# A banded-attention and two-block kernel on one core: the recorded list of order changes gets 59 more entries

## The chip, the cores and the metric

The kernel runs on one core of a Trainium2 chip. The time is the device time of one execution in microseconds (us), the median of several runs. The core has five engines with a queue of instructions each: TensorE (PE, matrix products), VectorE (DVE), ScalarE (ACT), GpSimd (POOL), and SyncE (SP), which here only starts transfers. An engine takes its own instructions in order. It stops at one whose input is not yet there, and everything behind that instruction waits too.

## The reference

Three steps follow each other for 4 batches of 576 positions and 512 channels (8 heads of 64).

```python
# 1. attention in a band of 128 positions, with a distance bias per head
scores = np.where(mask, scale * q @ k.T + bias, -1e9)      # mask: 0 <= i - j < 128
attn = exp(scores - max); attn /= sum;  x = attn @ v       # heads side by side: 512 channels
# 2. first block: 512 -> 1024 -> 512
h = maximum(x @ w_in, 0)
x = (h * sigmoid(conv3(h))) @ w_out                        # 3 taps per channel, centred
# 3. second block: 512 -> 512 -> 512
x = (sigmoid(conv5(x)) * (x @ w_val)) @ w_out2             # 5 taps per channel, causal
```

All data are fp32.

## The kernel before

**Tiling.** The work is cut into 8 units: each of the 4 batches has two parts of its positions (4 or 5 blocks of 64 rows in the first part). For a unit the steps are: attention, `hidden` (product with `w_in`, relu, 3-tap convolution, gate), `mixed` (product with `w_out` and the 5-tap convolution), `valued` (product with `w_val`, times the gate), `output` (product with `w_out2`). While one unit goes through the two blocks, the attention of the next is mixed in between. Channels lie on the 128 partitions, positions along the free axis, so that a tile is 128 x 254 to 128 x 322.

**Products of split numbers.** An fp32 matrix is held as a rounded "hi" part and the remainder "lo". A product is three matmuls: hi by hi, hi by lo, lo by hi (L1026, L1027, L1028; the first block of the later units uses halves of 16 bits, L1020). So every product needs its input split first. `cast` makes hi (L474 on ACT, L475 on DVE, L476 on POOL), `sub` makes lo (L508 on DVE, L509 on POOL).

**Work around the products.** Banded scores are matmuls (L802, L940). Then come a row minimum on DVE (L751), exp on ACT (L756), one over the row sum in two steps, a tiny one on POOL (L760) and a reciprocal on DVE (L762), a scaling of the rows (L817 POOL, L819 ACT, L823 DVE; in the later units L969 ACT or L971 DVE makes hi of it and L973 lo), a transposition (L829, or a transfer), and the product with v (L856, L1001). The taps of the convolutions are multiply-adds on DVE (L491), or a scaled copy on ACT (L501) that POOL adds (L502). `scaled` copies with a factor on ACT (L484) or DVE (L485). The weights come by transfers of 512 KB into a ring of three raw tiles and are unpacked by `widen`: L530 (DVE), L532 (ACT), L541 (DVE), then hi on ACT (L547) or POOL (L548) and lo on POOL (L509). A raw tile's next transfer can start only when its reader is through.

**What sets the order.** Each operation is entered once, with its inputs, outputs, length and the engines it may run on. A planner (`Program`, L84 to L260) then makes one order per engine: `forward` walks through the plan and gives each engine the ready operation of the smallest priority. `JOLTS` is a tuple of seeds. For each seed in turn `jolt` picks a stretch of 10, 30 or 60 us of the plan, adds random noise to the priorities of the operations in it, picks another engine for some of those that may run on several, changes how long some matmul groups of the attention are held back, and runs `forward` again. The result for one seed is the start of the next.

**Fillers.** Where the plan leaves PE free before 80 us, `warm` (L1239) puts small matmuls that nobody reads into PE's queue. Their number follows from the plan.

Of the kernel before, what the change touches and what calls it, by code (L numbers as in the profile page):

```python
# [37 lines left out]
NATIVE = ()  # L38
LATE = (11,)
HALF = {"in": 2, "out": 4}  # L40
# [1274 lines left out]
```

## Time and profile before

| | before |
|---|---|
| time, median of 3 runs | 402.96 us (402.84 to 403.02) |
| profiled execution: its own time | 402.0 us |
| profiled execution: span of the core | 400.2 us |
| PE busy | 385.5 us (96%), 3915 matmuls |
| DVE busy | 338.0 us (84%), 1041 instructions |
| ACT busy | 301.1 us (75%), 919 instructions |
| POOL busy | 239.3 us (60%), 365 instructions |
| granted TensorE clock | 1.00 in every stretch |

Busy shares are averages over the span. What matters for an order is the idle time: on which engine, at which place, and for whom the engine waited there. The number in square brackets in a timeline row is this idle time, with the instruction that ended it.

### The profile page before, as it was taken

Reading aid. Unit: us, or ns where it says so; the run is one execution under the profiler, and the core shown is the slowest. Engines: PE = TensorE matmul, PEld = TensorE weight load, DVE = VectorE, ACT = ScalarE, POOL = GpSimd, SP = SyncE. Lnnn points to the kernel's source line nnn. Section 1 sums busy time; section 2 is a strip of 40 time slices with the busy share of each in tenths; the row PEclk is TensorE's granted clock in tenths of the full one; section 3 lists DMA queues with packets and bytes.
Section 4 is the critical chain, followed back from the end, with each engine's and each line's share of the span. In section 5 each row is a group of like instructions: output and inputs, shape, how many; then the busy total and the mean of one; then the engine's idle time right before and its main releaser. Section 6 shows DMA issues by size and latency. Waiting matters only on the chain.

```text
span 400.2 us, 10946 instructions
## 1 busy us (share of the span) xinstructions
PE 385.5 (96%) x3915; PEld 336.3 (84%) x3915; DVE 338.0 (84%) x1041; ACT 301.1 (75%) x919; POOL 239.3 (60%) x365
## 2 busy tenths in 40 slices
PE   8898999999999998999999999999999999999996
PEld 7678988899998877999899866799878877798886
DVE  3999999999889989988879998986989778945591
ACT  4989999858797796758977987768877769714661
POOL 3677998947769737744476867353555248532631
PEclk9999999999999999999999999999999999999999
DMA  7977678753544474706692564707284620301001
GB/s 250 314 242 292 233 249 278 245 156 66 168 102 125 149 171 118 181 12 191 94 186 42 179 146 118 175 7 204 75 166 62 119 55 2 63 19 67 2 0 55
DMA packets 64919, 53.79 MB, mean 134 GB/s; under 512 B 44512, under 2 KB 57184, under 8 KB 64864
## 3 DMA queue, kind: packets, MB, share of 16 engines
q1 hardware_dynamic: 64864, 53.08, 49.2%
q8 instruction: 31, 0.51, 0.5%
q14 instruction: 24, 0.20, 0.2%
HBM read 38.51 MB, written 4.72 MB: 108 GB/s over the span
## 4 chain that ended last, share of the span: by engine, by line
PE 65%; DVE 16%; ACT 8%; DMA 5%; issue 3%; POOL 2%; SPq 1%; POOLq 0%; DVEq 0%; ACTq 0%
PE pm L1020 18%; PE pm L1026 13%; PE pm L1027 12%; PE pm L1028 12%; DVE t L491 4%; PE pss L940 3%; PE pss L1001 2%; DMA raw<-in_vN 2%; DVE pss L751 2%; DMA raw<-in_w_val 1%; PE pss L802 1%; DVE gts L491 1%; DVE gts L541 1%; DVE raw L530 1%; ACT pss L756 1%
## 5 line engine op out<-in xcount | busy, mean ns | idle before, releaser
L1020 PE MATMUL pm<-xh,hin 128*128 128x320 f16 (+1 forms) x504 | 68.5, 286 | 0.4 <-DVE t L491 0.3
L1020 PEld LDWEIGHTS <-hin 128*128 128x128 f16 x504 | 48.1, 97 | 14.6 <-issue 1.3
L1020 PEld LDWEIGHTS <-hout 128*128 128x128 f16 x384 | 37.0, 97 | 13.0 <-issue 2.1
L502 POOL TENSOR_TENSOR gts<-gts,t 128x317 f32<-128x317 f32 (+3 forms) x36 | 29.2, 820 | 28.6 <-ACT t L501 17.7
L1026 PE MATMUL pm<-g,wout 128*128 128x254 f32 (+3 forms) x128 | 39.4, 308 | 2.0 <-DVE t L491 1.5
L1026 PE MATMUL pm<-g,wval 128*128 128x318 f32 (+3 forms) x128 | 39.9, 312 | 0.6 <-ACT gts L1128 0.2
L1026 PE MATMUL pm<-g,wo 128*128 128x318 f32 (+3 forms) x128 | 39.3, 307 | 0.0
L1027 PE MATMUL pm<-g,wval 128*128 128x318 f32 (+3 forms) x128 | 38.1, 298 | 0.0
L1028 PE MATMUL pm<-g,wout 128*128 128x254 f32 (+3 forms) x128 | 37.8, 296 | 0.2 <-POOL wout L509 0.2
L1027 PE MATMUL pm<-g,wout 128*128 128x254 f32 (+3 forms) x128 | 38.0, 297 | 0.0
L1027 PE MATMUL pm<-g,wo 128*128 128x318 f32 (+3 forms) x128 | 37.9, 296 | 0.0
L1028 PE MATMUL pm<-g,wo 128*128 128x318 f32 (+3 forms) x128 | 37.7, 294 | 0.0
L1028 PE MATMUL pm<-g,wval 128*128 128x318 f32 (+3 forms) x128 | 37.6, 294 | 0.0
L751 DVE CUSTOM_DVE_ANT_0 pss<-pss,bm 128x192 f32<-128x192 f32 (+2 forms) x90 | 30.6, 349 | 7.3 <-PE pss L802 5.5
L756 ACT ACTIVATE pss<-pss,st 128x192 f32<-128x192 f32 (+2 forms) x81 | 30.3, 375 | 7.7 <-DVE st L751 7.1
L491 DVE SCALAR_TENSOR_TENSOR t<-pm,wcc,t 128x318 f32<-128x318 f32 (+3 forms) x56 | 28.3, 512 | 5.6 <-ACT t L484 3.6
L509 POOL TENSOR_TENSOR g<-gts,g 128x318 fp32r<-128x318 f32 (+3 forms) x26 | 21.3, 827 | 18.3 <-DVE g L475 9.2
L1077 ACT ACTIVATE t<-t 128x318 f32<-128x318 f32 (+3 forms) x64 | 28.4, 446 | 4.1 <-DVE t L491 3.6
L491 DVE SCALAR_TENSOR_TENSOR t<-t,pm 128x318 f32<-128x318 f32 (+3 forms) x64 | 28.3, 448 | 2.7 <-ACT t L1077 2.5
L973 DVE SCALAR_TENSOR_TENSOR pp<-pss,st,pp 128x192 f16<-128x192 f32 (+2 forms) x79 | 27.7, 388 | 2.0 <-ACT pp L969 1.6
L491 DVE SCALAR_TENSOR_TENSOR t<-pm,cc,t 128x254 f32<-128x254 f32 (+7 forms) x56 | 27.6, 511 | 0.7 <-ACT t L484 0.5
L1067 ACT ACTIVATE pm<-pm,wsc 128x320 f32<-128x320 f32 (+1 forms) x42 | 20.1, 478 | 10.1 <-PE pm L1020 9.7
(195 smaller groups left out, 1304.4 us busy)
## 6 DMA issues: line engine op xcount, KB each, us to landing
raw<-in_w_out SPq DMA_DIRECT2D x12, 512.0 KB, 4.2
raw<-in_w_in SPq DMA_DIRECT2D x8, 512.0 KB, 4.5
qkt<-in_qk SPq DMA_DIRECT2D x10, 384.0 KB, 4.1
vr<-in_vN SPq DMA_DIRECT2D x36, 96.0 KB, 3.0
qkt<-in_qk SPq DMA_DIRECT2D x6, 480.0 KB, 4.1
pp<-in_qk SPq DMA_DIRECT2D x6, 480.0 KB, 4.5
raw<-in_vN SPq DMA_DIRECT2D x6, 384.0 KB, 3.3
pp<-in_qk SPq DMA_DIRECT2D x6, 384.0 KB, 4.5
```

The source lines that it names most:

```text
L491: pg.add("DVE", dve_t(n, 0 if isinstance(scalar, float) else 1), lambda: nc.vector.scalar_tensor_tensor(out=out, in0=in0, scalar=scalar, i ...
L502: pg.add("POOL", pool_t(n, True), lambda: nc.gpsimd.tensor_tensor(out=out, in0=out, in1=t, op=ALU.add), prio, (tk,), (key,))
L509: "POOL": (pool_t(n, True), lambda: nc.gpsimd.tensor_tensor(out=lo, in0=src, in1=f32(hi), op=ALU.subtract))}
L751: pg.add("DVE", 75 + 1.05 * nkey, lambda: nc.vector.tensor_tensor_reduce(out=s, in0=s, in1=tab[:, 192 - nkey:192], op0=ALU.add, op1=ALU.mi ...
L756: pg.add("ACT", act_t(nkey, True, 2), lambda: nc.scalar.activation(out=to, in_=s, func=AF.Exp, scale=-1.0, bias=best, accum_out=total), pr ...
L973: pg.add("DVE", dve_t(nkey, 1), lambda sc=sc, hi=hi, lo=lo, ri=ri: nc.vector.scalar_tensor_tensor(out=lo, in0=sc, scalar=ri, in1=hi, op0=A ...
L1020: return [nc.tensor.matmul(out=o, lhsT=a, rhs=b_, start=first and i == 0, stop=last and i == 2) for i, (a, b_) in enumerate(((wh, hi), (wh ...
L1026: return [nc.tensor.matmul(out=o, lhsT=wh, rhs=hi, start=first, stop=False), nc.tensor.matmul(out=o, lhsT=wh, rhs=lo, start=False, stop=Fa ...
L1027: nc.tensor.matmul(out=o, lhsT=wh, rhs=lo, start=False, stop=False),
L1028: nc.tensor.matmul(out=o, lhsT=wl, rhs=hi, start=False, stop=last)]
L1067: pg.add("ACT", act_t(Nx, True, 1 if half else 0) + 35, lambda h=h: nc.scalar.activation(out=h[:, 0:Nx], in_=h[:, 0:Nx], func=AF.Relu, sca ...
L1077: pg.add("ACT", act_t(Ng), lambda c=c: nc.scalar.activation(out=c, in_=c, func=AF.Tanh, scale=0.5), pr, (), (ak,))
```

## The change

The tuple `JOLTS` gets 59 more seeds behind the 60 that it had. Nothing else in the file changes; later lines move down by 6 (L509 becomes L515, L760 becomes L766).

```diff
-    30003181, 30003414, 30003574, 30003667, 30003669)
+    30003181, 30003414, 30003574, 30003667, 30003669, 50000130, 50000253, 50000317, 50000349, 50000423, 50000450,
...
+    220004046)
```

The operations, tiles and transfers stay the same 2731. What changes is their order on each engine and, for some, the engine. Counting the built programs: ACT goes from 777 to 768 instructions, DVE from 1018 to 1031, POOL from 370 to 366, SP keeps 232. PE loses 20 fillers (111 to 91) and keeps every matmul that is read. The engines change for these operations:

| operation | before | after |
|---|---|---|
| `cast` ACT / DVE / POOL | 69 / 6 / 37 | 66 / 8 / 38 |
| `sub` DVE / POOL | 7 / 113 | 11 / 109 |
| hi of the row scaling, L969 ACT / L971 DVE | 89 / 15 | 84 / 20 |
| row scaling, L819 ACT / L817 POOL | 18 / 16 | 20 / 14 |
| hi of a weight, L547 ACT / L548 POOL | 14 / 10 | 13 / 11 |
| relu, L1067 ACT / L1069 DVE | 58 / 6 | 56 / 8 |

On PE 460 of 494 groups of matmuls keep their order among each other, and none moves by more than 6 places. The order is unchanged from 81 to 180 us and from about 320 to 330 us of the profiled execution of before.

Three places follow, each before and after. A row has the line, the kind, and output<-inputs with the shape.

**First place:** POOL at about 51 to 57 us of before, while the weights are unpacked and the second unit's attention starts. `st0` holds row sums, `pp` the exponentials, `wout` the weights `w_out`, `gts` what `widen` unpacks into, `x` the attention's output.

```order
L729 CAST x2_130<-x2_130 128x2x4
L729 CAST x3_131<-x3_131 128x2x4
L509 TENSOR_TENSOR wout140_89<-gts_141,wout040_81 128x512
L502 TENSOR_TENSOR t8_140<-t8_140,t0_132 128x253
L817 TENSOR_SCALAR pp_192<-pp_192,st0_190 128x192
L760 TENSOR_SCALAR st0_190<-st0_190 128x2
L548 TENSOR_SCALAR wout050_82<-gts_141 128x512
L760 TENSOR_SCALAR st0_190<-st0_190 128x1
L817 TENSOR_SCALAR pp_192<-pp_192,st0_190 128x192
L509 TENSOR_TENSOR g6_123<-t7_139,g6_123 128x254
L817 TENSOR_SCALAR pp_192<-pp_192,st0_190 128x192
L509 TENSOR_TENSOR wout150_90<-gts_141,wout050_82 128x512
```

```order
L735 CAST x2_130<-x2_130 128x2x4
L508 TENSOR_TENSOR t8_140<-t8_140,t0_132 128x253
L515 TENSOR_TENSOR wout140_89<-gts_141,wout040_81 128x512
L823 TENSOR_SCALAR pp_192<-pp_192,st0_190 128x192
L554 TENSOR_SCALAR wout050_82<-gts_141 128x512
L766 TENSOR_SCALAR st0_190<-st0_190 128x2
L515 TENSOR_TENSOR wout150_90<-gts_141,wout050_82 128x512
L823 TENSOR_SCALAR pp_192<-pp_192,st0_190 128x192
L766 TENSOR_SCALAR st0_190<-st0_190 128x1
L515 TENSOR_TENSOR g6_123<-t7_139,g6_123 128x254
```

The remainder of `wout150` moved up by four operations, and both tiny operations on `st0` moved behind a longer one.

**Second place:** POOL at about 288 to 298 us, in `hidden` and `mixed` of a later unit. `ghout` are the hi and lo halves of the gated hidden rows, `v16` and `vr` the values of the next attention (`vr` is filled by a transfer).

```order
L476 TENSOR_SCALAR v16_179<-vr_178 128x640
L760 TENSOR_SCALAR st1_191<-st1_191 128x6
L476 TENSOR_SCALAR ghout30_168<-t7_139 128x258
L908 TENSOR_TENSOR v16_179<-vr_178,v16_179 128x640
L509 TENSOR_TENSOR ghout30_168<-t7_139,ghout30_168 128x258
L509 TENSOR_TENSOR ghout40_169<-t0_132,ghout40_169 128x258
L502 TENSOR_TENSOR t3_135<-t3_135,t4_136 128x258
L509 TENSOR_TENSOR ghout50_170<-t1_133,ghout50_170 128x258
L509 TENSOR_TENSOR ghout60_171<-t2_134,ghout60_171 128x258
L905 TENSOR_SCALAR vr_178<-vr_178,vup_189 128x768
L509 TENSOR_TENSOR ghout70_172<-t3_135,ghout70_172 128x258
```

```order
L482 TENSOR_SCALAR v16_179<-vr_178 128x640
L515 TENSOR_TENSOR ghout20_167<-t6_138,ghout20_167 128x258
L914 TENSOR_TENSOR v16_179<-vr_178,v16_179 128x640
L515 TENSOR_TENSOR ghout30_168<-t7_139,ghout30_168 128x258
L482 TENSOR_SCALAR ghout40_169<-t0_132 128x258
L515 TENSOR_TENSOR ghout40_169<-t0_132,ghout40_169 128x258
L508 TENSOR_TENSOR t3_135<-t3_135,t4_136 128x258
L515 TENSOR_TENSOR ghout50_170<-t1_133,ghout50_170 128x258
L515 TENSOR_TENSOR ghout60_171<-t2_134,ghout60_171 128x258
L515 TENSOR_TENSOR ghout70_172<-t3_135,ghout70_172 128x258
L911 TENSOR_SCALAR vr_178<-vr_178,vup_189 128x768
```

The cast of `ghout30` left POOL for ACT, that of `ghout40` came from ACT, and the last `ghout` row stands ahead of the scaling of `vr`.

**Third place:** DVE at about 300 to 305 us, in `mixed`. `g6`, `g7`, `g8` are lo halves of the outputs, `gts` the sums of the 5-tap convolution, `pm1` to `pm3` the PSUM tiles of the products.

```order
L485 TENSOR_SCALAR gts_141<-pm2_195,wcc_188 128x258
L1121 SCALAR_TENSOR_TENSOR g6_123<-pm1_194,wcc_188,g6_123 128x258
L491 SCALAR_TENSOR_TENSOR gts_141<-pm1_194,wcc_188,gts_141 128x258 x2
L1121 SCALAR_TENSOR_TENSOR g7_124<-pm2_195,wcc_188,g7_124 128x258
L491 SCALAR_TENSOR_TENSOR gts_141<-pm2_195,wcc_188,gts_141 128x258
L491 SCALAR_TENSOR_TENSOR gts_141<-pm1_194,wcc_188,gts_141 128x258
L491 SCALAR_TENSOR_TENSOR gts_141<-pm2_195,wcc_188,gts_141 128x258
L1121 SCALAR_TENSOR_TENSOR g8_125<-pm3_196,wcc_188,g8_125 128x258
L491 SCALAR_TENSOR_TENSOR gts_141<-pm2_195,wcc_188,gts_141 128x258
L491 SCALAR_TENSOR_TENSOR gts_141<-pm3_196,wcc_188,gts_141 128x258
```

```order
L1127 SCALAR_TENSOR_TENSOR g6_123<-pm1_194,wcc_188,g6_123 128x258
L497 SCALAR_TENSOR_TENSOR gts_141<-pm1_194,wcc_188,gts_141 128x258
L1127 SCALAR_TENSOR_TENSOR g7_124<-pm2_195,wcc_188,g7_124 128x258
L497 SCALAR_TENSOR_TENSOR gts_141<-pm2_195,wcc_188,gts_141 128x258
L497 SCALAR_TENSOR_TENSOR gts_141<-pm1_194,wcc_188,gts_141 128x258
L497 SCALAR_TENSOR_TENSOR gts_141<-pm2_195,wcc_188,gts_141 128x258
L497 SCALAR_TENSOR_TENSOR gts_141<-pm1_194,wcc_188,gts_141 128x258
L497 SCALAR_TENSOR_TENSOR gts_141<-pm2_195,wcc_188,gts_141 128x258
L497 SCALAR_TENSOR_TENSOR gts_141<-pm3_196,wcc_188,gts_141 128x258
L1123 TENSOR_SCALAR g8_125<-pm3_196,wcc_188 128x258
L497 SCALAR_TENSOR_TENSOR gts_141<-pm3_196,wcc_188,gts_141 128x258
L1127 SCALAR_TENSOR_TENSOR g8_125<-pm3_196,wcc_188,g8_125 128x258
```

The scaled copy at the head left for ACT, and the lo half of `g8` moved behind the convolution sums of `pm1` and `pm2`; its hi half (L1123, before on ACT) came to DVE.

## Rows read from the trace of the kernel before

**Rows 1.** The page: busy time by engine, and the chain that ended last.
```profile
PE 385.5 (96%) x3915; PEld 336.3 (84%) x3915; DVE 338.0 (84%) x1041; ACT 301.1 (75%) x919; POOL 239.3 (60%) x365
PE 65%; DVE 16%; ACT 8%; DMA 5%; issue 3%; POOL 2%; SPq 1%; POOLq 0%; DVEq 0%; ACTq 0%
```
**Rows 2.** Windows: start:end, length, busy us (instructions) of five engines, clock, DMA.
```profile
20.00:74.00 54.00, 50.36 (x436) 44.92 (x436) 52.35 (x171) 50.42 (x149) 46.20 (x73) 1.00 0.77 260
```
**Rows 3.** Waits of DVE, 20 to 74 us: us in total, times, longest.
```profile
DVE raw L530 <- DMA raw<-in_w_val: 0.5, 1, 0.5
...
DVE pss L751 <- ACT pp L484: 0.3, 1, 0.3
DVE gts L541 <- POOL wout L509: 0.2, 1, 0.2
```
**Rows 4.** Timeline of POOL, 53 to 54.6 us: start us, length us, instruction.
```profile
53.12 0.43 POOL L817 TENSOR_SCALAR pp<-pp,st 128x192 f32<-128x192 f32 x1
53.64 0.19 POOL L760 TENSOR_SCALAR st<-st 128x2 f32<-128x2 f32 x1
53.91 0.62 POOL L548 TENSOR_SCALAR wout<-gts 128x512 fp32r<-128x512 f32 x1
```
**Rows 5.** Timeline of DVE, 54 us.
```profile
54.10 0.16 DVE L762 RECIPROCAL st<-st 128x2 f32<-128x2 f32 x1
```
**Rows 6.** Timeline of PE, 291 to 305 us.
```profile
291.49 0.38 PE L1020 MATMUL pm<-ghout,hout 128*128 128x258 f16 x2 [0.41 <-POOL ghout L509]
292.12 0.82 PE L1020 MATMUL pm<-ghout,hout 128*128 128x258 f16 x6 [0.25 <-DVE t L491]
...
296.77 1.93 PE L1020 MATMUL pm<-ghout,hout 128*128 128x258 f16 x14
...
304.07 0.28 PE L1028 MATMUL pm<-g,wval 128*128 128x258 f32 x1
304.48 0.39 PE L1026 MATMUL pm<-g,wval 128*128 128x258 f32 x1
```
**Rows 7.** Timeline of POOL, 289 to 297 us.
```profile
289.40 1.40 POOL L908 TENSOR_TENSOR v<-vr,v 128x640 f16<-128x640 f32 x1
290.76 1.31 POOL L509 TENSOR_TENSOR ghout<-t,ghout 128x258 f16<-128x258 f32 x2
...
296.06 0.91 POOL L905 TENSOR_SCALAR vr<-vr,vup 128x768 f32<-128x768 f32 x1 [1.78 <-DMA vr<-in_vN]
```
**Rows 8.** Timeline of DVE, 291 to 304 us.
```profile
291.65 0.42 DVE L491 SCALAR_TENSOR_TENSOR t<-t,pm 128x258 f32<-128x258 f32 x1
...
303.55 0.48 DVE L1121 SCALAR_TENSOR_TENSOR g<-pm,wcc,g 128x258 fp32r<-128x258 f32 x1
```
**Rows 9.** Timeline of PE, 371 to 374 us.
```profile
373.80 0.94 PE L1020 MATMUL pm<-ghout,hout 128*128 128x258 f16 x7 [0.20 <-DVE t L491]
```
**Rows 10.** Timeline of ACT, 380 us, reading PSUM tile pm1.
```profile
380.16 0.48 ACT L501 ACTIVATE t<-pm,wcc 128x258 f32<-128x258 f32 x1
```
**Rows 11.** Timeline of DVE, 380 us, reading the same tile pm1.
```profile
380.67 0.48 DVE L485 TENSOR_SCALAR gts<-pm,wcc 128x258 f32<-128x258 f32 x1 [3.40 <-ACT t L501]
```
**Rows 12.** Waits of DVE, 262 to 293 us.
```profile
DVE st L762 <- POOL st L760: 1.7, 2, 1.2
DVE t L491 <- ACT t L484: 1.4, 2, 1.2
DVE psx L751 <- PE psx L940: 1.2, 1, 1.2
```
**Rows 13.** Timeline of DVE, 273 to 275 us.
```profile
273.88 0.68 DVE L971 TENSOR_SCALAR pp<-pss,st 128x128 f16<-128x128 f32 x2
```
**Rows 14.** Groups of PE by line: busy us, mean ns of one, idle before them.
```profile
L1239 PE MATMUL psx<-one 128*128 128x192 bf16 x111 | 13.1, 267 | 1.1 <-DVE one L1166 1.1
```
**Rows 15.** Timeline of DVE: a sub beside POOL's work, and one alone.
```profile
333.37 0.81 DVE L508 TENSOR_TENSOR ghin<-t,ghin 128x318 f16<-128x318 f32 x1
...
392.24 0.43 DVE L508 TENSOR_TENSOR g<-gts,g 128x258 fp32r<-128x258 f32 x1 [0.49 <-ACT g L474]
```
**Rows 16.** Timeline of POOL, 333 us.
```profile
333.04 0.79 POOL L509 TENSOR_TENSOR ghin<-t,ghin 128x318 f16<-128x318 f32 x1
```

5 rows, old and new, of the table JOLTS are left out of this document.

## The prediction

> **What bounds the kernel now.** I read the page first. PE is busy for 96% of the span, and the chain that ended last runs over PE for 65% and over DVE for 16% [rows 1]. All matmuls that are read stay, at a granted clock of 1.00. So a new order can win only where PE stands still or runs fillers, and it can lose where it makes PE wait anew.
>
> Next come the windows. From 20 to 74 us DVE works 52.35 of 54 us [rows 2]. Here PE and the fillers leave room, but DVE, which unpacks the weights and feeds the attention, is the engine that sets the pace. An order gains there only what DVE idles, some 1.65 us. The waits of DVE in this stretch say for what: 0.5 us for a transfer of `w_val`, 0.3 for ACT's scaled copy, 0.2 for POOL's remainder of a weight [rows 3].
>
> After 180 us PE is nearly always busy, and the timeline of PE shows single pauses of 0.2 to 0.4 us, each with an engine that ended it [rows 6, 9]. Those are the places to look up in the two orders. The longest pauses after 74 us lie either in the unchanged part, or behind waits whose order stays; I count nothing for them.
>
> **The change part by part.**
>
> *Start-up, 20 to 74 us.* The three waits of DVE in the rows are all touched. ACT's copy, L484, stands five places earlier. POOL's remainder of `wout150` stands four places earlier. The transfer of `w_val` waits for a DVE reader of its ring tile, and that reader now stands three places earlier in DVE's queue. If all three waits go, that is 0.5 + 0.3 + 0.2 = 1.0 us of a queue that is otherwise full.
>
> Against this stands POOL's tiny L760. It began at 53.64 [rows 4], and DVE's reciprocal that needs it at 54.10 [rows 5], so 0.27 us of slack were left behind its end at 53.83. Now a scaling of 0.43 more and the 0.62 of L548 stand in front of it [rows 4]. If POOL comes to this place as late as before, L760 ends at 53.83 + 0.43 + 0.62 = 54.88 and DVE waits 54.88 - 54.10 = 0.78 us. If POOL comes earlier, since the tap ahead of it no longer stands behind a remainder that had to wait, the price goes to 0. Behind the waiting reciprocal the whole unpacking queues on DVE. I take 0.5, nearer to the upper end, because POOL is also busy for 46.20 of the 54 us [rows 2]. Sum: -1.0 + 0.5 = **-0.5 us**, bounds -1.0 and +0.78 (no wait removed, the full new one).
>
> *291 to 292 us.* PE pauses for 0.41 us until POOL has made the lo half `ghout30`, and 0.25 us more for a multiply-add of DVE [rows 6]. POOL came late because the cast of `ghout30` was its own and L908 took 1.40 us between the cast and the remainder [rows 7]. Now the cast is ACT's and one POOL operation is gone from the queue: 0.4 us earlier, so the first pause goes. What is late next is DVE's multiply-add from 291.65 to 292.07 [rows 8], which PE needs for the following group; it depends on DVE's own queue, so the second pause may grow into the room. Of the two pauses, 0.66, I count **-0.43**; bounds 0 and -0.66.
>
> *297 us.* Fourteen matmuls take 1.93 us from 296.77; by the groups of two (0.38) and of six (0.82) one more takes (0.82 - 0.38) / 4 = 0.11, so fourteen need 0.38 + 12 x 0.11 = 1.70 [rows 6]. The 0.23 too much is the last `ghout` remainder, which stood behind the scaling of `vr`, and this had waited 1.78 us for its transfer [rows 7]. It now stands ahead: **-0.22**, bounds 0 and -0.23.
>
> *304 us.* The matmul at 304.48 starts 0.41 after the one before it, where 0.12 is the step [rows 6]: 0.29 of waiting for DVE's convolution sum. The lo half of `g8`, 0.48 us on DVE [rows 8], stood before the sums and now stands behind them, and a scaled copy has left for ACT: **-0.29**, bounds 0 and -0.29. This is hidden again if `g8` itself is then the last to come; its hi half is now on DVE too.
>
> *372 to 374 us.* A pause of 0.20 us for DVE [rows 9]. A tap on POOL stands two places earlier, and two remainders and a cast came from POOL and ACT to DVE: **-0.20**, bounds -0.35 and +0.3.
>
> *380 us.* DVE's scaled copy begins at 380.67 [rows 11], 0.03 us after ACT ends with the same PSUM tile [rows 10]: the two engines take turns on a tile. In the new order another instruction of ACT on that tile, which was DVE's, is queued first. DVE then starts up to 0.4 later, and the chain behind it feeds PE in `valued`. Bounds 0 and +0.4, taken in the middle: **+0.20**.
>
> *268 to 290 us, at no cost.* Here DVE gets some 2.5 us more: a remainder (0.43) [rows 15], five hi rows of the attention at about 0.34 (two in 0.68) [rows 13] and a scaled copy (about 0.4). I let it cost nothing, because DVE waits 1.7, 1.4 and 1.2 us in this stretch [rows 12], 4.3 in all. If that cover is gone, it costs up to 2.5 (a rival below). The other moves (0 to 20, 188 to 205, 259 to 262 and 384 to 395 us) shift work between engines with no PE pause next to them: 0.
>
> *Sum:* -0.5 - 0.43 - 0.22 - 0.29 - 0.20 + 0.20 = **-1.44 us**. It is made against the profiled execution of 402.0 us, of which 400.2 are the span; that execution is 0.96 below the median of 402.96. I carry the difference over to the median: 402.96 - 1.44 = **401.5 us**.
>
> *A rule against this change.* The sub on DVE beside POOL's work took 0.81 us from 333.37, with POOL's own sub running from 333.04 to 333.83; alone it took 0.43, on a somewhat narrower tile [rows 15, 16]. So next to POOL a moved sub can cost 0.38 more. The Trainium skill ("SBUF — State Buffer", section "Who interferes with whom") says why: a DVE instruction with two inputs in SBUF and a GpSimd instruction that reads SBUF share a port pair, and one blocks the other for its whole length. By that rule the trace agrees at 333 us, and it speaks against the four subs that go to DVE.
>
> **The rivals.**
>
> *No change that can be measured.* The reciprocals wait the full 0.78 us and the three start-up waits come back in another form, because the DVE instructions that they depend on lie behind the waiting one. The late gains of 0.43 + 0.22 + 0.29 + 0.20 - 0.20 = 0.94 stay: 402.96 + 0.78 - 0.94 = 402.8. For it: DVE's queue holds the same work up to the matmul at 74 us, so only its idle time can go. Against it: the waits named in [rows 3] have causes that moved the right way.
>
> *Slower.* At 268 to 290 us DVE's waits are not spare time, as they end a chain (PE's scores, ACT's exp, POOL's L760, then the reciprocal), and the 2.5 us added come on top of it. `hidden` then reaches its multiply-adds late, and PE stands there. That takes the place of the gain at 291: 402.96 - 0.5 - 0.22 - 0.29 - 0.20 + 0.20 + 2.5 = 404.5. It decides from about 1 us that isn't covered. Against it: the waits are 4.3 us in all [rows 12], and PE's pauses there were 0.41 and 0.25 only.
>
> *A larger gain.* The plan needs 20 fillers fewer, at 13.1 / 111 = 0.118 us each [rows 14], that is 2.4 us that PE no longer has to bridge before 80 us. If the chip follows, -2.4 takes the place of -0.5: 402.96 - 2.4 - 0.94 = 399.6. Against it: DVE, not PE, sets the pace there, with 1.65 us idle [rows 2]; so I give it little.
>
> *The ports.* Two of the subs on DVE stand at 372 to 374 us on the path to PE. At 0.38 more each the 0.20 gained there becomes 0.56 lost: 401.5 + 0.76 = 402.3.
>
> That the change does nothing is excluded: the built orders differ at all these places.
>
> **How the numbers follow.** A measurement of this kernel can tell about 0.2%, 0.8 us, from no change. Chances: my forecast (401.5, own range 400.9 to 402.1) 0.38; no change (402.8) 0.26; larger gain (399.6) 0.15; slower (404.5) 0.15; the ports (402.3) 0.06. Faster by over 0.8 us means below 402.16: the forecast, the larger gain and a third of the ports, 0.38 + 0.15 + 0.02 = 0.55. Slower by over 0.8 means above 403.76: 0.15, and 0.01 of the no-change case if other reciprocals wait as well. Same: 0.29. For 8 in 10 the range runs from 399.7, which cuts half of the larger gain, to 404.0, which cuts most of the slower case.
>
> **What would show it.** In the profile of the changed kernel: the waits of DVE from 20 to 74 us no longer list the transfer of `w_val` and list the reciprocal behind POOL with about 0.5 us; the last matmul of the start-up stretch, fed by DVE, comes 0.5 us earlier; PE's pauses at 291, 297 and 304 us are gone or under 0.2 us; the copy at 380 us starts some 0.4 us later against its neighbours. I am wrong if PE reaches 180 us no earlier than before, or 1.5 us or more earlier, or if DVE from 268 to 290 us runs late into a new pause of PE.

## The result

The changed kernel takes 398.45 us (median of 6 runs, 397.7 to 398.82), the kernel before 402.9 us (median of 6 runs): ratio 0.9892, 95% interval 0.9871 to 0.9914. In a second set of runs the ratio was 0.9915 (0.9885 to 0.9945). By these two ratios the new order is 3.4 to 4.4 us faster, where 1.4 was forecast, and the time lies below the stated range. The sign was right, the size was not.

The page of the changed kernel, the lines that answer to [rows 1], with the line of the DMA queue that carries instructions:

```profile
PE 381.6 (96%) x3895; PEld 333.5 (84%) x3895; DVE 341.6 (86%) x1054; ACT 299.1 (76%) x910; POOL 237.3 (60%) x361
q8 instruction: 30, 0.49, 0.5%
PE 72%; DVE 10%; ACT 9%; POOL 3%; issue 2%; DMA 2%; ACTq 0%; POOLq 0%
```

The same line of the page before:

```profile
q8 instruction: 31, 0.51, 0.5%
```

The chain runs more over PE (72% against 65%) and less over DVE (10 against 16%). The packets of queue q8 are 16 KB each; before there are 31 in the span, now 30. They turn out to matter.

**Where the time came from.** All matmuls that are read are in both traces, so the start of the same group of matmuls can be compared from place to place. This table is worked out from the start times: how much a stretch (in us of the first profile of before) is shorter (-) or longer (+) than in that profile. The 13 other profiles, of the experiments below, stand beside it. "Fillers" counts the fillers, "order" says where the new order is used.

| profile | fillers | order new | 4-12 | 12-80 | 147-162 | 232-248 | 288-310 | 340-355 | 366 to last matmul |
|---|---|---|---|---|---|---|---|---|---|
| `before_again` | 111 | nowhere | -0.06 | +0.71 | -0.74 | +0.05 | -0.14 | +0.02 | +0.03 |
| `new_0_15` | 109 | to 15 | -0.04 | -0.14 | +0.65 | -0.95 | +0.27 | +0.02 | +0.01 |
| `new_264_329` | 111 | 264-329 | +0.13 | -0.22 | 0.00 | +0.12 | -1.24 | -0.01 | +0.01 |
| `new_329_end` | 111 | from 329 | -0.36 | -0.18 | +0.37 | -0.04 | -0.06 | -0.32 | -0.46 |
| `late_only` | 111 | from 134 | +0.13 | +0.07 | +0.45 | -0.94 | -1.24 | -0.33 | -0.47 |
| `after_111` | 111 | everywhere | -0.31 | -0.32 | +0.78 | -0.02 | -1.24 | -0.32 | -0.42 |
| `fillers_91` | 91 | nowhere | +0.85 | -0.08 | +0.29 | -0.94 | -0.43 | -0.01 | +0.32 |
| `fillers_71` | 71 | nowhere | -0.25 | +0.88 | -1.31 | -0.94 | -0.52 | +0.02 | 0.00 |
| `early_only` | 91 | to 134 | -0.09 | -0.40 | -0.65 | -0.94 | +0.90 | +0.02 | +0.18 |
| changed kernel | 91 | everywhere | -0.97 | -0.35 | -0.90 | -0.94 | -1.23 | -0.33 | -0.11 |
| `after_again` | 91 | everywhere | -0.50 | +0.11 | -0.83 | -0.94 | -1.24 | -0.31 | -0.13 |
| `after_71` | 71 | everywhere | -0.60 | +0.92 | -0.88 | -0.95 | -1.24 | -0.31 | -0.45 |
| `after_51` | 51 | everywhere | -0.17 | +2.41 | -1.09 | -0.95 | -1.24 | -0.30 | -0.45 |

Three things are to be read here. At 288 to 310, and at 340 to 355 us, the columns follow the order: -1.24 and -0.31 wherever it is new, in every profile. Where the order is old, 288 to 310 us varies from -0.52 to +0.90; the reason is given below, at 291 to 304 us. The two columns before, 147 to 162 and 232 to 248 us, are some 0.9 us shorter in the changed kernel. There they don't follow the order but, mostly, the number of fillers, although the fillers all lie before 80 us. The first column changes from execution to execution. Stretches left out changed by less than 0.3 us, but for 80 to 147 us in `new_329_end` (+1.17), 215 us in `after_again` (+0.6) and 264 us in `after_51` (+1.0).

The table ends with the last matmul. Behind it the new order loses 0.3 us: from the start of the last matmul to the end of the span it takes 3.48 to 3.50 us in all seven profiles with the old end, 3.78 to 3.80 in all seven with the new one. With this loss, and some 0.2 us of the stretches left out, the row of the changed kernel comes to the -4.3 us by which its span is shorter (395.9 against 400.2).

**What stands at 150 us.** Here the order on all engines is the same. DVE waits for a transfer of the values, before and after (timeline of DVE, idle time in brackets):

```profile
150.84 1.22 DVE L578 TENSOR_REDUCE vmx<-raw 128x4 f32<-128x1024 f32 x1 [1.76 <-DMA raw<-in_vN]
```
```profile
148.65 1.22 DVE L584 TENSOR_REDUCE vmx<-raw 128x4 f32<-128x1024 f32 x1 [0.86 <-DMA raw<-in_vN]
```

The transfer queue of SP shows why it is late, before and after (start, length of the issue):

```profile
144.47 1.59 SPq L901 DMA_DIRECT2D vr<-in_vN  x1
146.15 1.25 SPq L577 DMA_DIRECT2D raw<-in_vN  x2
```
```profile
143.17 0.48 SPq L907 DMA_DIRECT2D vr<-in_vN  x1
143.74 1.26 SPq L583 DMA_DIRECT2D raw<-in_vN  x2
145.04 2.15 SPq L907 DMA_DIRECT2D vr<-in_vN  x2
```

Before, the issue of one small transfer takes 1.59 us where 0.48 is usual, and the transfer for which DVE waits stands behind it. After, the long issue comes behind that transfer. In the DMA view of the 1.7 us from 144.2 before, and of the 1.5 us from 144.8 after, there is one packet of the instruction queue:

```profile
q8 instruction: 1, 0.02, 4.8%
```
```profile
q8 instruction: 1, 0.02, 5.1%
```

**What stands at 240 us.** Before, the product with v waits for the last transposed piece (timeline of PE):

```profile
238.33 0.87 PE L1001 MATMUL pss<-pp,v 64*64 64x64 f16 x48
239.95 0.53 PE L1001 MATMUL pss<-pp,v 64*64 64x64 f16 x24 [0.75 <-DMA pp<-pp]
```

After, it runs in one piece:

```profile
236.33 1.21 PE L1007 MATMUL pss<-pp,v 64*64 64x64 f16 x72
```

There was such a 16 KB packet here too: in the seven profiles with 111 or 109 fillers it began 0.3 to 0.6 us before the product, beside the last packets of the transposition, which landed 6.0 to 6.2 us after its issue in the five profiles with the wait and 4.5 to 4.8 us in the other nine; in the profiles with 91 it began 0.1 us before the product or later, and with 71 or 51 there was none in the six us ahead of it.

### The profile page after: what moved, and what is told of

It is laid out like the page before. It is cut to its first block, busy times and chain, and to the rows that moved or that the text cites. A ratio compares the mean times of both kernels' runs of the same rounds, so it can differ in the third digit from the quotient of the medians.

```text
span 395.9 us, 10906 instructions
## 1 busy us (share of the span) xinstructions
PE 381.6 (96%) x3895; PEld 333.5 (84%) x3895; DVE 341.6 (86%) x1054; ACT 299.1 (76%) x910; POOL 237.3 (60%) x361
## 4 chain that ended last, share of the span: by engine, by line
PE 72%; DVE 10%; ACT 9%; POOL 3%; issue 2%; DMA 2%; ACTq 0%; POOLq 0%
PE pm L1026 21%; PE pm L1032 14%; PE pm L1033 13%; PE pm L1034 13%; DVE t L497 4%; PE pss L946 4%; PE pss L1007 2%; DMA raw<-in_vN 1%; ACT pp L762 1%; DVE gts L497 1%; ACT pss L762 1%; ACT pm L1073 1%; ACT t L507 1%; PE pss L808 1%; PE psx L1245 1%
## 5 line engine op out<-in xcount | busy, mean ns | idle before, releaser
L515 POOL TENSOR_TENSOR g<-gts,g 128x318 fp32r<-128x318 f32 (+3 forms) x24 | 19.8, 835 | 15.1 <-ACT g L480 11.8
L1032 PEld LDWEIGHTS pm<-g,wout 128*128 128x128 f32 x128 | 24.1, 188 | 5.1 <-DVE t L497 2.4
```

Source lines behind the costliest of these rows:

```text
L515: "POOL": (pool_t(n, True), lambda: nc.gpsimd.tensor_tensor(out=lo, in0=src, in1=f32(hi), op=ALU.subtract))}
L1032: return [nc.tensor.matmul(out=o, lhsT=wh, rhs=hi, start=first, stop=False), nc.tensor.matmul(out=o, lhsT=wh, rhs=lo, start=False, stop=Fa ...
```

## The experiments

The kernels that mix the two orders make both plans and splice them where both have done the same set of operations. The changed lines are these, with the stretches of the new order in `TAKE` (places in the list of the 2731 operations):

```diff
-        for seed in JOLTS:
+        for i, seed in enumerate(JOLTS):
             new, out = self.jolt(seed)
             self.best = new
-        for o, h in self.best[1].items():
-            o.eng, o.dur, o.fn, o.start, o.end = h
+            if i == 59:
+                first, how = out, new[1]
+        return self.splice(first, how, out, self.best[1])
+
+    def splice(self, first, how1, last, how2):
+        out, at = [], 0
+        for lo, hi in TAKE + ((len(last), len(last)),):
+            for src, how, x, y in ((first, how1, at, lo), (last, how2, lo, hi)):
...
```

The fillers follow from the starts in the spliced plan. The theories that the expectations name: A, the three waits of 4, 150 and 240 us are chance of one execution; B, they belong to the order; C, they follow from the length of PE's program, which the fillers change; D, only the order matters, not the fillers.

**The same kernels again.** `before_again` and `after_again` are the two kernels without an edit.

> The kernel before, unchanged, for a second profile. In the first two profiles the stretches with an unchanged order lose three waits for transfers: the second batch of scores at 4 us (about 0.9 us later in before), DVE's minimum over raw<-in_vN at 150 us (1.76 us of waiting against 0.86) and the product with v at 240 us (0.75 us for pp<-pp against none). Theory A (these waits are chance of one execution): the second profile of the same kernel shows at least two of the three smaller, and its span is 1 to 2.5 us under 400.2. Theory B (they belong to the order): all three stand again within 0.2 us, span 400 to 401. Ratio 1.000 in both.

Ratio 0.9996 (0.9977 to 1.0014), span 400.4 us. The wait at 240 us stood again (0.80 us), the one at 150 us was 1.02 instead of 1.76 us. Neither A nor B in full.

> The changed kernel, unchanged, for a second profile. Theory A: some of the three waits (4, 150, 240 us) come back and the span is 0.5 to 2 us above 395.9. Theory B: they stay away, span 395.5 to 397. Ratio 0.987 to 0.991 in both.

Ratio 0.9915 (0.9885 to 0.9945), span 397.3 us. At 150 and 240 us the waits stayed away (0.93 us and none). Of the 1.4 us more span 0.5 lie in the first 12 us and 0.5 at 12 to 80.

**Only the early or only the late part new.**

```diff
+TAKE = ((0, 1000),)       # early_only, up to 134 us
+TAKE = ((1000, 2731),)    # late_only, from 134 us
```

> The new order up to about 120 us, the old one behind it (the cut lies in the stretch where the two are the same). Theory A: faster by 0.4 us (what the two first profiles differ by from 13 to 74 us), ratio 0.999. Theory B: the 4 us and the 150 us place go with the new order in front, 0.4 + 0.9 + 0.9 = 2.2 us, ratio 0.9945.

Ratio 0.9959 (0.9943 to 0.9975), that is 1.65 us, most of it not in the early stretch itself (-0.40 from 12 to 80 us) but at 150 and 240 us, where this kernel has the old order.

> The old order up to about 120 us, the new one behind it. Theory A: the pauses at 291, 297, 304 and 347 us go and 0.1 is lost around 380 us, 0.56 + 0.23 + 0.43 + 0.31 - 0.1 = 1.4 us faster, ratio 0.9965. Theory B: also the wait at 240 us goes, 2.4 us faster, ratio 0.994; the wait at 150 us stays.

Ratio 0.9937 (0.9913 to 0.9962), 2.5 us. The two effects, 1.65 and 2.5, add up to 4.2 us, as much as the whole change. So two causes are likely, and the one of the early part acts late. The sum is not a clean one, though: in the profile of `late_only` 0.94 us lie at 240 us, a wait that it escaped too.

**The number of fillers alone.**

```diff
-        while t + (90.0 if t < COLD + 1500.0 else 250.0) < end:
+        while len(filled) < 91 and t + (90.0 if t < COLD + 1500.0 else 250.0) < end:
```

> The order of before, unchanged, but the last 20 of the 111 fillers are left out (they lie from about 67 to 74 us), so that PE's program is as long as that of the changed kernel. The traces have one 16 KB packet of the queue named instruction about every 13 us; its place follows PE's program (the mean distance is 253 matmuls and weight loads), and a transfer that SP issues beside it takes 1.0 to 1.9 us to issue instead of 0.45. Theory C (20 fillers fewer shift these packets, and what they hit changes): the issue that takes over 1 us near 145 us moves behind raw<-in_vN, DVE's wait there falls from 1.8 to 0.9 us, and the kernel is 0.8 to 1.6 us faster, ratio 0.996 to 0.998, without any change of order. Theory D (fillers don't matter, only the order): ratio 0.9995 to 1.001.

Ratio 0.9965 (0.9945 to 0.9985): 1.4 us faster with the order of before, word for word. Its page says `q8 instruction: 30`, as that of the changed kernel. The profiled execution itself took 402.0 us, as before: it lost 0.85 us at 4 to 12 us, the stretch that changes from execution to execution. Of the two waits it was not the one expected that went: at 150 us DVE waited 2.03 us for the transfer, although the packet now lay behind its issue; at 240 us the wait was gone. Timelines of DVE and PE of this run:

```profile
151.91 1.22 DVE L578 TENSOR_REDUCE vmx<-raw 128x4 f32<-128x1024 f32 x1 [2.03 <-DMA raw<-in_vN]
```
```profile
239.38 1.21 PE L1001 MATMUL pss<-pp,v 64*64 64x64 f16 x72
```

The same edit with 71:

> The order of before with 71 fillers: another 20 fewer than in the run with 91, all behind the 71st left out. Theory C (the place of the 16 KB packets decides): with 91 the packet near 238 us fell 0.5 us later beside the work and the wait of 0.8 us for pp<-pp was gone; with 71 it falls later still, so this wait stays away; ratio 0.995 to 0.998. Theory D (the 91 run was chance): 0.9995 to 1.001. If the missing fillers let PE's clock fall, it shows in the granted clock and costs more than 1 us.

Ratio 0.9944 (0.9923 to 0.9964): 2.3 us faster, again without any change of order. Here both waits shrank, the one at 240 us to none and the one at 150 us to 0.43 us:

```profile
150.15 1.22 DVE L578 TENSOR_REDUCE vmx<-raw 128x4 f32<-128x1024 f32 x1 [0.43 <-DMA raw<-in_vN]
```

It also shows what the fillers are for. In the window from 40 to 60 us the granted clock was 0.91, a mean of the two levels of 2.4 and 1.2 GHz, after fillers behind the 71st were left out and PE stood still in their place:

```profile
40.00:60.00 20.00, 17.16 (x136) 15.28 (x136) 18.34 (x60) 18.06 (x51) 18.38 (x29) 0.91 0.72 227
```

By the starts of the matmuls this cost 1.5 us between 52 and 56 us. Another 0.7 were won back at 66 us, so that 12 to 80 us grew by 0.88. The sum alone would not show the clock: `before_again` lost 0.71 us in the same stretch, 0.6 of it at 66 us, with a granted clock of 1.00.

**The other way round:** the new order with 111 fillers.

```diff
-            nc.tensor.matmul(out=ps_x.t[0][:, 320:512], lhsT=junk[:, 0:128], rhs=junk[:, 0:192], ...
+            for c in (96, 96) if len(filled) < 40 else (192,):
+                nc.tensor.matmul(out=ps_x.t[0][:, 320:320 + c], lhsT=junk[:, 0:128], rhs=junk[:, 0:c], ...
...
+                filled.append(1)
```

The 20 fillers are added here at the start of the program, in the first 15 us; in `fillers_91` they are left out at their far end, which the profile of before shows at 51 to 71 us, not at 67 to 74 as I had expected. So it is the number of fillers that the two runs have in common, not the place.

> The changed order with 111 fillers instead of 91: the first 20 are split into two of half the columns, in the stretch up to 15 us, where PE waits for its first inputs anyway. Theory C: part of the gain is lost, the packets return to the places of before, 0.8 to 1.6 us slower than the changed kernel, ratio to before 0.993 to 0.996. Theory D: ratio 0.990 to 0.9915, as the changed kernel.

Ratio 0.9933 (0.9909 to 0.9957), slower than the changed kernel by 0.7 to 1.7 us by the two ratios of that kernel; the intervals overlap. The profile is clearer: 31 packets, and both waits are back, 2.53 us at 150 us and 0.74 us at 240 us (timeline of PE):

```profile
240.34 0.53 PE L1007 MATMUL pss<-pp,v 64*64 64x64 f16 x24 [0.74 <-DMA pp<-pp]
```

**Fewer fillers with the new order.** The cap of `fillers_91`, with 71 and 51, in the changed kernel.

> The changed order with 71 fillers instead of 91. Theory C: the packets shift again, other transfers are hit or spared; anywhere from 1 us faster to 1 us slower than the changed kernel, ratio 0.987 to 0.993, and the profile shows the two waits of 150 and 240 us by where the packets lie. Theory D: the same as the changed kernel within 0.1%.

Ratio 0.9907 (0.9887 to 0.9928), median 398.46 us: the same as the changed kernel.

> The changed order with 51 fillers. As with 71: theory C allows 1 us to either side of the changed kernel, ratio 0.987 to 0.993; theory D the same as the changed kernel. Without fillers from about 24 us on the clock may fall in the pauses of the start-up; then it is slower by more than 1 us and the granted clock shows it.

Ratio 0.9954 (0.9925 to 0.9983): slower than the changed kernel, by about 1 us by the medians (399.59 against 398.45 and 398.66), by 1.6 and 2.5 us by the ratios. The granted clock was 0.91 from 20 to 60 us, and the stretch from 12 to 80 us took 2.4 us more. No version that I ran beats the changed kernel.

**The parts of the order.**

```diff
+TAKE = ((0, 98),)         # new_0_15
+TAKE = ((1925, 2370),)    # new_264_329
+TAKE = ((2370, 2731),)    # new_329_end
```

> The new order only up to 15 us; 109 fillers. There only the scalings of rows change places between POOL and ACT. In the profiles so far PE stands at 11.7 us 0.99, 0.50, 0.30 and 0.09 us earlier with the new start, and between 0.84 us later and 0.36 earlier with the old one. Theory A (these differences are chance of the first transfers): ratio 0.9995 to 1.0005. Theory E (the new scalings save half a microsecond): 0.9985 to 0.999.

Ratio 1.0015 (0.9994 to 1.0037). The new start gains nothing; the first column of the table is chance of the first transfers.

> The new order only from 264 to 329 us of before; 111 fillers. By the prediction's steps the pauses at 291, 297 and 304 us go: 0.43 + 0.22 + 0.29 = 0.94 us, ratio 0.9977. By what the first profiles differ there: 0.56 + 0.23 + 0.44 = 1.2 us, ratio 0.997. If DVE's 2.5 us more are not covered at 268 to 290 us: slower, over 1.001.

Ratio 0.9959 (0.9943 to 0.9975), 1.65 us (1.0 to 2.3). In the profile the stretch is 1.24 us shorter, as in all others with this order.

> The new order only from 329 us to the end; 111 fillers. By the prediction's steps: -0.20 at 372 us and +0.20 at 380, ratio 1.000. By the first profiles: 0.31 at 347, 0.2 lost at 372, 0.28 lost at 380 and 0.55 won at 386 us, 0.4 us in all, ratio 0.999.

Ratio 0.9994 (0.9977 to 1.0011). The profile shows -0.32 and -0.46 us; 0.30 of these 0.78 us are lost again behind the last matmul. The runs can't tell the 0.5 us that are left from nothing. (This profile also lost 1.17 us once before 147 us.)

## Why the prediction was right or wrong

**The step that failed** is the sentence on the pauses after 74 us: those in the unchanged part, or behind waits whose order stays, I counted as nothing, so that they would remain. Two of them went, 0.9 us each in the first profile of the changed kernel. A fixed order of instructions does not fix where the packets of the instruction queue fall. Removing 20 fillers takes 40 instructions out of PE's program, and with 51 to 91 fillers the late transfers were hit less:

| wait, in the profiles | 111 or 109 fillers (7) | 91 or fewer (7) |
|---|---|---|
| DVE for `raw<-in_vN` at 150 us | 1.76, 1.02, 2.39, 2.19, 1.75, 2.13, 2.53 (mean 1.97) | 2.03, 0.43, 1.09, 0.86, 0.93, 0.86, 0.67 (mean 0.98) |
| PE for `pp<-pp` at 240 us | 0.75, 0.80, none, none, 0.88, 0.71, 0.74 | none in all seven |

The difference of the means is 1.0 us at the first place, where the two groups overlap, and 0.55 at the second (3.88 / 7), 1.5 together; the timed run `fillers_91` gave 1.4 us. This is half or more of the 2.0 to 3.0 us that the forecast missed; 0.3 us more came at 291 to 304 us and 0.3 at 347 us. I had seen that 20 fillers are gone, and priced them as time of PE only. My own sign of being wrong came true: PE reached the work of 180 us 2.2 us earlier in the first profile of the changed kernel, where 1.5 was the limit (1.2 in the second), and 1.0 of it had come before 12 us.

**The rival with the larger gain** named 399.6 us, the nearest to the result, from the right count of fillers. That is luck: its mechanism did not happen. DVE sets the pace of the start-up, as the forecast said, and 12 to 80 us shrank by 0.35 us, not by 2.4.

**Start-up, -0.5.** About right: -0.35 in the changed kernel, -0.40 in `early_only`, -0.32 in `after_111`, +0.11 in `after_again`. But with an unchanged order the stretch varied from -0.22 to +0.71 in the profiles with 111 fillers, so the profiles can't confirm half a microsecond. The two halves were both smaller than I put them. The waits of [rows 3] are gone in this profile, and others came, 0.3 for POOL's tap; in `after_again` DVE waited 0.7 us for a transfer of `w_out`. Waits of DVE, and the window between the same two matmuls as in [rows 2], of which the first starts 1.0 us earlier, after:

```profile
DVE pss L757 <- PE pss L808: 0.3, 1, 0.3
DVE gts L497 <- POOL gts L508: 0.3, 1, 0.3
```
```profile
19.00:72.70 53.70, 49.07 (x418) 43.48 (x418) 52.60 (x171) 50.89 (x150) 46.38 (x73) 1.00 0.79 263
```

DVE now idles 1.10 us (53.70 - 52.60) against 1.65 [rows 2], 0.55 less where I had 1.0, and it works 0.25 us more. The reciprocal that I feared to wait 0.5 us waited for next to nothing. POOL reached L766 earlier, since the tap and the remainder ahead of it had changed places; timelines of POOL and of DVE:

```profile
52.88 0.19 POOL L766 TENSOR_SCALAR st<-st 128x2 f32<-128x2 f32 x1
```
```profile
53.10 0.17 DVE L768 RECIPROCAL st<-st 128x2 f32<-128x2 f32 x1
```

I had taken the value nearer the wrong end.

**291 to 304 us, -0.94.** The mechanism was right in all three steps, the size too small: -1.24 in every profile. The timeline of PE after, which answers to [rows 6]:

```profile
288.61 1.48 PE L1026 MATMUL pm<-ghout,hout 128*128 128x258 f16 x12 [0.31 <-DVE t L497]
...
292.28 3.90 PE L1026 MATMUL pm<-ghout,hout 128*128 128x258 f16 x34
...
299.60 0.36 PE L1032 MATMUL pm<-g,wval 128*128 128x258 f32 x1
```

Of the two pauses at 291 one of 0.31 for DVE is left. That place gave 0.56 (0.43 forecast), the one at 297 us 0.23 (0.22), the one at 304 us 0.44 (0.29).

The place at 297 us hides more than these 0.23 us. In the old order POOL's last `ghout` remainder stands behind the scaling of `vr`, so PE depends there on when that transfer lands. POOL waited for it from 1.01 us (`fillers_71`) to 2.67 us (`early_only`), and in `early_only` PE stood still behind it (timelines of POOL and of PE):

```profile
295.04 0.91 POOL L923 TENSOR_SCALAR vr<-vr,vup 128x768 f32<-128x768 f32 x1 [2.67 <-DMA vr<-in_vN]
```
```profile
296.64 1.59 PE L1038 MATMUL pm<-ghout,hout 128*128 128x258 f16 x13 [0.96 <-POOL ghout L527]
```

These two are the ends of the -0.52 to +0.90 in the table. The new order takes PE off this transfer, and its seven profiles agree within 0.01 us.

**268 to 290 us at no cost.** Right, and the slower rival with it wrong: PE stayed busy for all of 259 to 288 us, and DVE's waits shrank to take the new work up ([rows 12] before). Window and waits after:

```profile
259.00:288.00 29.00, 29.00 (x323) 26.03 (x323) 25.81 (x93) 22.68 (x76) 13.93 (x23) 1.00 0.41 105
```
```profile
DVE psx L757 <- PE psx L946: 1.2, 1, 1.2
DVE t L497 <- ACT t L490: 0.6, 1, 0.6
DVE st L768 <- POOL st L766: 0.6, 1, 0.6
```

**372 us, -0.20:** it came in `late_only`, `new_329_end`, `after_71`, `after_51` and `after_111` (-0.2 to -0.3), and not in the two profiles of the changed kernel (+0.15). The two profiles with 91 fillers and the old order lost there too (+0.3 in `fillers_91`, +0.17 in `early_only`), so this place as well goes with the fillers. **380 us, +0.20:** right, +0.28. The pause before the first group of `valued` stayed and grew to 0.41 us:

```profile
380.62 0.36 PE L1032 MATMUL pm<-g,wval 128*128 128x258 f32 x1 [0.41 <-DVE gts L497]
```

Two gains I had overlooked: 0.31 at 347 us, where the pauses ahead of groups of `valued` shrank, and 0.55 at 387 us. I had looked at the pauses with a releaser in the timeline, and these are spread over several matmuls.

**The ports.** The subs that came to DVE cost nothing extra. The one beside POOL's sub was 0.81 again, and it was there before; a moved one, next to a POOL instruction that began after it, took 0.42:

```profile
369.33 0.42 DVE L514 TENSOR_TENSOR ghout<-t,ghout 128x258 f16<-128x258 f32 x1
```

The Trainium skill ("SBUF — State Buffer", section "Who interferes with whom") says that whoever issues first gets the shared ports. The trace agrees as to who waits: 0.81 at 329 us behind a POOL sub already running, and 0.42 at 369 us ahead of POOL's cast. The losses were smaller than the whole overlap, though. At its own width of 318 a sub of DVE takes 0.49 (at 268.82 us), so the one at 329 us lost 0.32 of the 0.47 us that POOL still ran, not the 0.38 of my forecast; POOL's cast at 369 us took 0.52 instead of 0.41, a loss of 0.11 of 0.25. The new order has no moved sub behind a running one.

**What stays open.** That the number of fillers moves the packets and the two waits is shown by the profiles of `fillers_91` against `before` and of `after_111` against the changed kernel; in `fillers_91` nothing differs from before but PE's fillers. That the packets carry PE's program is argued, not shown: 31 packets on 7830 matmuls and weight loads make 253 each, 20 fillers fewer make 30 packets, and in `fillers_91` they lie at nearly the same places of PE's program as in the changed kernel. Whether a packet near a transfer delays it depends on more than its time. In `fillers_91` DVE waited 2.03 us at 150 us with the packet in a good place, and `late_only` and `new_0_15` escaped at 240 us with it in a bad one. I did not find what decides there.

## What to carry to other kernels

A tuned order depends on things outside the order. Before a change of order is credited with a gain, run the old order with the new program length, and look whether the gain lies in stretches that the change did not touch. Count the instructions of the engine with the longest program: adding or removing a few dozen on PE shifted the packets of the instruction queue here, and 1 to 2 us hung on it. Pauses that are ended by an engine just ahead in the chain could be forecast from the trace to 0.15 us each at 291, 297 and 304 us; those that hung on a transfer were not foreseen.

## What the runs showed of the hardware

Queue q8 moved one 16 KB packet about every 13 us (31 in 400 us), each 0.9 to 1.5 us long in most cases. A transfer that SP issued during one often took long to issue: counted from the starts in the 14 profiles (from 15 us on, transpositions left out), 90 of the 216 issues that overlap a packet took over 0.8 us, up to 2.1, and 1 of the 2130 others did (median 0.43). The places in the program where this happened repeated within one or two transfers between executions of a kernel and moved with the number of fillers.

Fewer fillers on PE were free only to a point. With 71 the granted clock fell to 0.91 in one stretch of 20 us, with 51 in two. The start-up took 0.9 and 2.4 us longer in these profiles; in the old order with 71 (`fillers_71`) the gains at 150, 240 and 297 us were larger than that.
